# Attention and a feed-forward network on one core: which FFN work lies beside which attention work while the weights are converted

## The chip, the cores and the metric

The kernel runs on one core of a Trainium2 chip. The metric is the device time of one execution in microseconds (us). Matmuls run on TensorE (PE; PEld is its loading of weights); elementwise work on VectorE (DVE), ScalarE (ACT) and GpSimd (POOL); SyncE (SP) issues the DMA transfers.

## The reference

Eight batches of eight heads with 576 tokens of 64 dimensions go through an attention that is causal by blocks of 64 tokens. The result, 4608 tokens of 512 values, goes through two matrix products with a leaky ReLU between them.

```python
scores = scale * np.matmul(q, k.transpose(0, 1, 3, 2))
mask = block_i >= block_j                 # blocks of 64
scores = np.where(mask, scores, -1000000000.0)
attn = np.exp(scores - max) / (sum + 1e-09)
x = (attn @ v).transpose(0, 2, 1, 3).reshape(4608, 512)
h = x @ w_in                              # 512 x 2048
g = np.maximum(0.01 * h, h)
return g @ w_out                          # 2048 x 512
```

q, k and v come as fp32. The weights come as float64, 8 bytes a value, and the kernel makes fp32 of them by integer operations.

## The kernel before, in words

**Split products.** To keep fp32 exactness at the rate of the faster type fp32r, a matrix is cut into a high and a low part, each fp32r, and a product becomes three: high by high, high by low, low by high. The weights have the parts wih, wil, woh and wol; the FFN's input has xh and xl; its middle values have gh and gl; the keys have kh and kl, the probabilities pth and ptl. "Casting" below is making a high part (one copy, L274 on ACT or L275 on DVE), "subtracting" making a low part (L284 on DVE, L285 on POOL).

**Weights.** 64 pieces of 256 columns go through `weight_piece` (L360-419): a load of 8-byte words into one of six `raw` buffers, then steps on `val`, one of six: ACT or DVE scales the upper word, DVE shifts (L397) and ors in the lower word (L401), the sign comes by DVE (L406) or, for every third piece, by ACT and POOL (L410, L411), and a cast and a subtraction give the two parts.

**Attention** (`attention`, L421-665) handles 72 work items. Batch 0 makes 16 of them: items 0 to 7 are its heads' tokens 0 to 319 ("lo"), items 8 to 15 the tokens 320 to 575 ("hi"). From item 16 an item is a whole head ("full"); items 16 to 23 are batch 1. An item loads q, k and v; PE makes scores in the two banks of PSUM called p_s (plain fp32 products L488 for items 0 to 14, the split ones L494 from item 15; every second lo item uses the p_h banks); DVE sets masked corners (memset, L505) and takes maxima (L512, nm), ACT the exponentials (L521, prow), then sums, reciprocals (L535, L536, rec) and normalising (L549 POOL, L550 DVE, L551 ACT); PE transposes the probabilities through the two p_t banks (L573), from which pth and ptl are made; the products with v go back into p_t (L625 plain, L635 split), and copies and adds (L614, L663) put them into xr, the FFN's input by batch. xr of batch 1 lies in memory that the conversion leaves, so it exists only when all weights are there.

**FFN.** 18 chunks of 256 tokens, each in 8 units of 256 columns of the hidden layer. `ffn1` (L723-743) makes 24 matmuls of 256 columns into p_h (L734), then ACT's g (L741), its cast gh and the subtraction gl. `ffn2` (L745-771) makes 12 matmuls of 512 columns into p_o (L753), two banks that sum over all eight units; after the last unit p_o is copied to ob (L770) and stored by SP. Chunk 0 needs the lo items of batch 0, chunk 1 the hi items as well, chunk 2 all of batch 1.

**Order.** No loop fixes the order. Every step is given to `Plan` (L63-234) with its possible engines and their costs, a rank (the number of the item plus an offset of that step's kind) and the buffers that it reads and writes. `Plan.run` plays the program through with its own costs; each engine takes the ready step of lowest rank, and the order that comes out is the program. PE has two rules of its own. A group of transposes ("short") and half an ffn2 unit ("long") that are both ready are put into each other, one matmul of the one, one of the other; and a group of transposes that has no such partner lets other PE work go first for up to PATIENCE ns. Where PE has nothing while work of rank below 12 is open, the plan puts in filler matmuls that nobody reads (L806, 81 of them, two records each).

Chunks 0 and 1 follow one another by rank: chunk 0 spread over items 8 to 15, chunk 1 over 16 to 23, each unit as a step of the items' count. The conversion's ranks run from OFF1 over SL1, also counted in items. Chunk 1's units thereby lie between the scores, transposes and products of batch 1.

Of the kernel before, what the change touches and what calls it, by code (L numbers as in the profile page):

```python
# [17 lines left out]
P = 128  # L18
# [7 lines left out]

HS = 7
SIGNS = 3

WIDE = 256  # L30
RAWS = 6
VALS = 6

RL = 7.153
RP = 0.885
RB = 0.516
RT = 1.485
RV = 1.932
RX = -0.113
RN = -0.908  # L40

LEAD = 1.751
LAG = 1.627
RS = 0.514
RG = -0.26
OFF1 = 4.574
SL1 = 11.938
AHEAD = -0.663

LAT = 1550  # L50
HOLD = 567.499

PATIENCE = 424.599
FILL = 235
# [8 lines left out]
class Plan:  # L63


# [36 lines left out]
    def run(self):  # L102
# [12 lines left out]
        order, now, moved, done = [], 0, 0, 0  # L115
        load, start, stream = -LOAD, 0, 0

# [15 lines left out]

        def multiply(matmuls):
            nonlocal load, start, stream
            for cost, fn in matmuls:
                if now < SLOW:
                    cost *= 2
                load = max(load + LOAD, start, now - 57)
                start = max(start + stream, load + 57, now)  # L140
                stream = cost
                order.append(fn)
            return start + stream

        def best(kind):
            found = [x for x in ready["PE"] if self.ops[x[1]][4] == kind and not ends[x[1]]]
            return min(found) if found else None

# [3 lines left out]
        while done < total:  # L152
# [6 lines left out]
            for e, q in ready.items():  # L159
                while q and ends[q[0][1]]:  # L160
                    heapq.heappop(q)
                if not q or free[e] > now:
                    continue
                other = {"DVE": "POOL", "POOL": "DVE"}.get(e)
                if other:
                    open_ = port[other] <= now
                    can = [x for x in q if not ends[x[1]] and (open_ or (e == "DVE" and self.ops[x[1]][0][x[2]][0] == "DVE"))]
                    if not can:
                        wake.append(port[other])
                        continue  # L170
                    x = min(can)
                    q.remove(x)
                    heapq.heapify(q)
                elif e == "PE":
                    live = [x for x in q if not ends[x[1]]]
                    x = min(live)
                    short, long_ = best("short"), best("long")
                    if self.ops[x[1]][4] == "short" and not long_:
                        other_ = [y for y in live if self.ops[y[1]][4] != "short"]
                        if other_ and now < since[x[1]] + PATIENCE:  # L180
                            x = min(other_)
                    kind = self.ops[x[1]][4]
                    if kind == "long":
                        self.fill = None
                    if kind in ("short", "long") and short and long_:
                        a = [(c, f, short[1]) for c, f in self.ops[short[1]][0][0][1]]
                        b = [(c, f, long_[1]) for c, f in self.ops[long_[1]][0][0][1]]
                        mixed = []
                        while a or b:
# [4 lines left out]
                        at = {}  # L194
                        for c, f, i in mixed:
                            at[i] = multiply([(c, f)])
                        free[e] = start + stream
                        for y in (short, long_):
                            q.remove(y)
                            end(y[1], e, at[y[1]])  # L200
                        heapq.heapify(q)
                        continue
                    q.remove(x)
                    heapq.heapify(q)
                    free[e] = multiply(self.ops[x[1]][0][x[2]][1])
# [12 lines left out]
                order.append(fn)  # L218
                end(i, e, moved + LAT if lag else free[e])
# [38 lines left out]
def attention_ffn(ctx: ExitStack, tc: tile.TileContext, qk: bass.AP, v: bass.AP, w_in: bass.AP, w_out: bass.AP, out: bass.AP):  # L258
# [73 lines left out]
    p_h = fixed([P, 2, CH], F32, "p_h", 2, pool=psum)  # L332
    p_o = fixed([P, DM], F32, "p_o", 2, pool=psum)

# [86 lines left out]
    def attention(i):  # L421
# [10 lines left out]
        sk = "h" if odd else "s"  # L432

        def scored(k):
            return p_h[k].rearrange("p a b -> p (a b)") if odd else p_s[:, k, :]

# [125 lines left out]
        if kind != "lo":  # L562
            softmax(
                [(4, p_s[:, :, 0:288], (0, 1))],
                [(k, (4, p_s[:, k, 0:288], 288 * k, 288 * k + 288, c)) for k in range(2) for c in range(1 if plain_s else 2)],
                [p_s[0:64, 1, 224:288]], r0 + RB,
            )
        for base, c0, w, items in tgroups[kind]:
            x = bank()

            def transpose(t, j, c, x=x):
                n = P if kind == "full" else qn[t]
                return RATE * n, lambda: nc.tensor.transpose(p_t[x][:, c : c + n], row(t, n, j * P, P), ident[:n, :n])  # L573

            add([("PE", [transpose(*y) for y in items])], r0 + RT, [k for t in sorted({a for a, _, _ in items}) for k in pkeys(t)], [("t", x)], kind="short")
            src = p_t[x][:, c0 : c0 + w]
# [128 lines left out]

    def split_x(c, rank):
        at = c * CH
        while at < (c + 1) * CH:
# [13 lines left out]

    def ffn1(c, u, rank):  # L723
        ks = [(a, d) for a in ("xh", "xl") for d in range(0, CH, BLK)]
        hh = p_h[u % 2]
        z = u % 2
        for i in range(2):
            f = 2 * u + i

            terms = [(w, x, d) for d in range(ND) for w, x in ((wih, xh), (wih, xl), (wil, xh))]  # L730

            def go(k, i=i, f=f, terms=terms):
                w, x, d = terms[k]
                nc.tensor.matmul(  # L734
                    hh[:, i, :], w[:, d, f * P : (f + 1) * P], x[:, d, :], start=k == 0, stop=k == len(terms) - 1
                )
# [7 lines left out]

    def ffn2(c, u, rank):  # L745
        z = u % 2
        for m in range(2):

            terms = [(a, w, i) for a, w in ((gh[z], woh), (gh[z], wol), (gl[z], woh)) for i in range(2)]

            def go(k, m=m, terms=terms):
                a, w, i = terms[k]
                nc.tensor.matmul(  # L753
                    p_o[m], a[:, i, m * P : (m + 1) * P], w[:, 2 * u + i, :],
                    start=u == 0 and k == 0, stop=u == NU - 1 and k == 5,
                )

            add(
                [("PE", [(RATE * DM, lambda k=k, go=go: go(k)) for k in range(6)])], rank + m / 1000,
                [("gh", z), ("gl", z)] + wkeys[("wo", 2 * u)] + wkeys[("wo", 2 * u + 1)], [("o", m)], kind="long",  # L760
            )
            if u == NU - 1:
# [6 lines left out]

                add(copying(512, lambda buf=buf: buf, lambda m=m: p_o[m], sb=False), rank, [("o", m)], [key])  # L770
                add([("SP", 475, store)], rank, [key], [("out", c, m)], lag=dma(P * DM * 4))
# [13 lines left out]
    for i in range(len(work) + 1):  # L785
        if i in events:
            here = [c for c in range(NCHUNK) if ready[c] == i]
            nxt = events[events.index(i) + 1] if i != events[-1] else i + H
            num = len(here) * NU
            for k in range(num):  # L790
                c, u = here[k // NU], k % NU
# [3 lines left out]
                ffn1(c, u, rank)  # L795
                ffn2(c, u, rank + (nxt - i) * LAG / num + 0.003)
        if i == 2 * H:
# [5 lines left out]
    if FILL:  # L803

        def fill():
            nc.tensor.matmul(p_o[0][:, 0:P], ident, ident, start=True, stop=True)  # L806

# [29 lines left out]
```

## Time and profile before

| | |
|---|---|
| median of 3 runs | 1193.65 us (1190.58 to 1194.34) |
| profiled execution | 1194.37 us, its span 1192.3 us |
| granted TensorE clock, mean | 0.996 |
| busy: PE, DVE, ACT, POOL | 99%, 57%, 55%, 36% of the span |
| HBM read and written | 64.57 MB and 9.44 MB |

The span is the time from the first to the last recorded instruction; 2.1 us of the execution lie around it. A row of the timeline has start, duration, engine, line, operation, the tiles written and read, shapes and the count of equal instructions, with the idle time of the engine before it in brackets. Matmuls are pipelined: a record is longer than the time from one start to the next. A row of the groups has the count, busy time, mean duration in ns, and after the second bar the idle time in front of them. A row of the windows has the stretch, its length, the busy time of PE, weight loads, DVE, ACT and POOL with their counts, the granted clock, the busy share of the DMA engines and GB/s.

### The profile page before, as it was taken

The page shows a single profiled execution, that of the slowest core. Times are in us where ns is not written, and L with a number is a line of the kernel's source. Part 1 is how long each engine was busy: PE and PEld are TensorE (multiplying, and loading weights), DVE is VectorE, ACT ScalarE, POOL GpSimd, SP SyncE. Part 2 cuts the span into 40 slices and gives each one's busy share as a digit, 9 for nine tenths or more (in the row PEclk, how much of TensorE's full clock was granted, in tenths as well). Part 3 has the DMA queues.
Part 4 walks back from the last instruction along what each step waited for, and adds up shares of the span by engine and source line. Part 5 has one row for each costly group of instructions (what it writes and reads, how often), then busy time and mean ns, then how long its engine had stood idle before and what let it go on. Part 6 is the DMA issues. An engine that isn't in the chain of part 4 may idle for free.

```text
span 1192.3 us, 21079 instructions
## 1 busy us (share of the span) xinstructions
PE 1175.5 (99%) x7778; PEld 1041.4 (87%) x7778; DVE 680.2 (57%) x1782; ACT 657.4 (55%) x1652; POOL 431.5 (36%) x505
## 2 busy tenths in 40 slices
PE   9999899899999999999999999999999999999998
PEld 7877789788899988898999988898998888899997
DVE  5999987766656666644444456665666666310000
ACT  6988866655655565554554455555555555422222
POOL 3233344324443443423332343443444343212222
PEclk9999999899999999999999999999999999999999
DMA  6656422211212111110211211112121210000000
GB/s 175 185 173 193 128 88 72 66 60 55 67 51 70 52 55 60 37 64 30 62 39 35 67 49 55 47 51 69 52 69 46 70 31 30 1 18 1 18 19 18
DMA packets 39592, 75.37 MB, mean 63 GB/s; under 512 B 4032, under 2 KB 23040, under 8 KB 39488
## 3 DMA queue, kind: packets, MB, share of 16 engines
q1 hardware_dynamic: 39488, 74.02, 20.2%
q8 instruction: 61, 1.00, 0.3%
q14 instruction: 43, 0.35, 0.1%
HBM read 64.57 MB, written 9.44 MB: 62 GB/s over the span
## 4 chain that ended last, share of the span: by engine, by line
PE 96%; DVE 2%; ACT 1%; DMA 0%; issue 0%; ACTq 0%; DVEq 0%
PE p_o L753 33%; PE p_h L734 33%; PE p_t L573 9%; PE p_t L635 8%; PE p_s L494 8%; PE p_t L625 2%; PE p_s L488 2%; PE p_o L806 2%; DVE nm L512 1%; PE p_h L488 0%; DVE ptl L284 0%; DVE prow L550 0%; DMA qk_in<-in_qk 0%; ACT prow L521 0%; DMA raw<-in_w_in 0%
## 5 line engine op out<-in xcount | busy, mean ns | idle before, releaser
L285 POOL TENSOR_TENSOR gl<-g,gh 128x512 fp32r<-128x512 f32 x136 | 176.8, 1300 | 460.6 <-ACT gh L274 311.3
L734 PE MATMUL p_h<-xh,wih 128*128 128x256 f32 x1152 | 323.2, 281 | 0.0
L734 PE MATMUL p_h<-xl,wih 128*128 128x256 f32 x1152 | 320.1, 278 | 1.1 <-DVE xl L284 1.1
L734 PE MATMUL p_h<-xh,wil 128*128 128x256 f32 x1152 | 319.9, 278 | 0.0
L521 ACT ACTIVATE prow<-p_s,nm 128x192 f32<-128x192 f32 (+4 forms) x308 | 161.8, 529 | 151.4 <-DVE nm L512 95.4
L573 PE MATMUL p_t<-ident,prow 128*128 128x128 f32 x960 | 239.7, 274 | 3.1 <-DVE ptl L284 0.9
L734 PEld LDWEIGHTS p_h<-xl,wih 128*128 128x128 f32 x1152 | 216.9, 188 | 4.6 <-DVE xl L284 1.3
L734 PEld LDWEIGHTS p_h<-xh,wih 128*128 128x128 f32 x1152 | 216.9, 188 | 4.5 <-issue 1.0
L753 PE MATMUL p_o<-wol,gh 128*128 128x512 f32 x576 | 219.9, 453 | 0.0
L734 PEld LDWEIGHTS p_h<-xh,wil 128*128 128x128 f32 x1152 | 217.0, 188 | 0.0
L741 ACT ACTIVATE g<-p_h 128x512 f32<-128x512 f32 x144 | 85.7, 595 | 234.4 <-PE p_h L734 234.1
L753 PE MATMUL p_o<-woh,gh 128*128 128x512 f32 x576 | 204.0, 426 | 0.0
L753 PE MATMUL p_o<-woh,gl 128*128 128x512 f32 x576 | 192.2, 415 | 0.0
L549 POOL TENSOR_SCALAR prow<-prow,rec 128x192 f32<-128x192 f32 (+4 forms) x214 | 119.1, 568 | 167.1 <-DVE rec L536 124.3
L284 DVE TENSOR_TENSOR ptl<-p_t,pth 128x512 fp32r<-128x512 f32 (+1 forms) x224 | 125.1, 567 | 63.0 <-ACT pth L274 59.6
L614 DVE TENSOR_TENSOR xr<-p_t,xr 64x64 f32<-64x64 f32 x112 | 50.4, 450 | 164.6 <-ACT xr L274 164.3
L573 PEld LDWEIGHTS p_t<-ident,prow 128*128 128x128 f32 x960 | 130.2, 141 | 13.9 <-DVE ptl L284 1.9
L512 DVE TENSOR_REDUCE nm<-p_s 128x1 f32<-128x192 f32 (+4 forms) x308 | 139.7, 486 | 4.6
L753 PEld LDWEIGHTS p_o<-wol,gh 128*128 128x128 f32 x576 | 108.6, 188 | 35.6
L753 PEld LDWEIGHTS p_o<-woh,gh 128*128 128x128 f32 x576 | 105.5, 189 | 28.1 <-issue 2.6
L274 ACT CAST pth<-p_t 128x384 fp32r<-128x384 f32 (+3 forms) x175 | 81.5, 469 | 63.9 <-PE p_t L573 59.5
L753 PEld LDWEIGHTS p_o<-woh,gl 128*128 128x128 f32 x576 | 96.6, 189 | 20.0
(77 smaller groups left out, 1623.9 us busy)
## 6 DMA issues: line engine op xcount, KB each, us to landing
qk_in<-in_qk SPq DMA_DIRECT2D x56, 576.0 KB, 3.7
v_stage<-in_v SPq DMA_DIRECT2D x56, 160.0 KB, 2.2
out<-ob SPq DMA_DIRECT2D x35, 256.0 KB, 2.0
raw<-in_w_in SPq DMA_DIRECT2D x32, 256.0 KB, 3.0
raw<-in_w_out SPq DMA_DIRECT2D x32, 256.0 KB, 3.2
qk_in<-in_qk SPq DMA_DIRECT2D x8, 160.0 KB, 3.0
vf<-in_v SPq DMA_DIRECT2D x8, 160.0 KB, 3.2
vf<-in_v SPq DMA_DIRECT2D x8, 128.0 KB, 2.6
```

The lines of the kernel that those rows point to most:

```text
L274: one = lambda: nc.scalar.copy(dst(), src())
L284: ("DVE+" if sb else "DVE", dve(n), lambda: nc.vector.tensor_sub(dst(), one(), two())),
L285: ("POOL", pool2(n), lambda: nc.gpsimd.tensor_sub(dst(), one(), two())),
L494: go = lambda ap=ap, cols=cols, kk=kk, k0=k0, k1=k1, first=first, last=last: nc.tensor.matmul(ap, qs[z][:, cols], kk[:, k0:k1], start=firs ...
L512: [("DVE", dve(kw[t]), lambda t=t, ap=ap, flat=flat: nc.vector.tensor_reduce(nm[z][: qn[t], t : t + 1], ap[: qn[t]], axis=AX.X if flat els ...
L521: nc.scalar.activation(o, ap[: qn[t]], AF.Exp, bias=nm[z][: qn[t], t : t + 1], scale=1.0, accum_out=sums[z][: qn[t], t : t + 1])
L549: ("POOL", pool1(kw[t]), lambda: nc.gpsimd.tensor_scalar(p(), p(), by, 1.0, op0=ALU.mult, op1=ALU.mult)),
L573: return RATE * n, lambda: nc.tensor.transpose(p_t[x][:, c : c + n], row(t, n, j * P, P), ident[:n, :n])
L635: nc.tensor.matmul(to, vs[z][:, j, :], src, start=start, stop=stop)
L734: nc.tensor.matmul(hh[:, i, :], w[:, d, f * P : (f + 1) * P], x[:, d, :], start=k == 0, stop=k == len(terms) - 1)
L741: add([("ACT", act(512), lambda: nc.scalar.activation(g, hh, AF.Prelu, alpha=0.01))], rank, [("h", z)], ["g"])
L753: nc.tensor.matmul(p_o[m], a[:, i, m * P : (m + 1) * P], w[:, 2 * u + i, :], start=u == 0 and k == 0, stop=u == NU - 1 and k == 5,)
```

## The change

The weights' pieces become 512 columns wide, 32 of them, with three buffers of each kind in place of six; every second one takes its sign from ACT and POOL. The scores of batch 0, in plain fp32 for all 16 items, go into p_o, which is one tile of two banks now; its q and k loads fill all 128 partitions (the inputs hold each row twice), with half the scale, since each product is then summed twice. Chunk 0 sums in p_s instead, takes its split input from space in pth and kl, and so can run while batch 0's last scores use p_o. Chunks 0 and 1 run in step: unit k of chunk 0, then unit k-6 of chunk 1, with ranks tied to the conversion and not to the items. From chunk 2 on the loop is as before, with other offsets. PE takes its lowest rank always: transposes are no longer put between the matmuls of ffn2 and stay together as a group. The planner's second choice of an engine (a cast on DVE, say, where ACT is the first) is allowed after 59 ns in place of 567.

```diff
-HS = 7
-SIGNS = 3
-WIDE = 256
-RAWS = 6
-VALS = 6
+HS = 8
+SIGNS = 2
+WIDE = 512
+RAWS = 3
+VALS = 3
...
+JOINL = 6.278
+LATER = 6
+JOIN = -0.606
+JLAG = 1.738
...
-HOLD = 567.499
-
-PATIENCE = 424.599
+HOLD = 59.027
...
-                    if kind in ("short", "long") and short and long_:
...
-                            if b:
-                                mixed.append(b.pop(0))
-                            if a:
-                                mixed.append(a.pop(0))
...
+                    x = heapq.heappop(q)
...
-    p_o = fixed([P, DM], F32, "p_o", 2, pool=psum)
+    p_o = fixed([P, 2, DM], F32, "p_o", pool=psum)
...
-        rows = D if plain_s else P
+        rows = P
...
+        p_k = p_s if kind == "full" else p_o
...
-            add(copying(qe - qa, lambda: q_in, lambda: q_in, by=scale), rp, [], [qkey])
+            add(copying(qe - qa, lambda: q_in, lambda: q_in, by=scale / 2), rp, [], [qkey])
...
     def split_x(c, rank):
+        if c == 0:
+            x = xr[0][:, :, c * CH : (c + 1) * CH]
+            keys = [("x", 0, h, 0) for h in range(H)]
+            hi = [("pth", y[0]) for y in tgroups["full"]]
+            add(copying(4 * CH, lambda: x2h, lambda: x, first="DVE"), rank, keys, hi)
+            for y in range(2):
+                ds = slice(2 * y, 2 * y + 2)
+                add(subtracting(2 * CH, lambda y=y: x2l[y], lambda ds=ds: x[:, ds], lambda ds=ds: x2h[:, ds]), rank, keys + hi, [("kl", y)])
+            return
...
+            po, po_key = (p_s[:, m, :], ("s", m)) if c == 0 else (p_o[:, m, :], ("o", m))
...
+            if i == 2 * H:
+                steps = [y for k in range(NU + LATER) for y in ((0, k), (1, k - LATER)) if 0 <= y[1] < NU]
+                for k, (c, u) in enumerate(steps):
+                    rank = OFF1 + SL1 * (u + 1) / NU + JOIN + c * JOINL
+                    if u == 0:
+                        split_x(c, (c + 1) * H + JOINX)
+                    ffn1(c, u, k % 2, rank)
+                    ffn2(c, u, k % 2, rank + JLAG)
+                here = []
+            if i == H:
+                here = []
...
-            nc.tensor.matmul(p_o[0][:, 0:P], ident, ident, start=True, stop=True)
+            nc.tensor.matmul(p_s[:, 0, 0:P], ident, ident, start=True, stop=True)
```

By the lines moved, L488 becomes L460, L494 L466, L573 L545, L625 L597, L635 L607, L734 L722, L753 L741, L512 L484, L521 L493, L274 and L275 L245 and L246, L284 and L285 L255 and L256. In the program's order, the lists per engine of before and after, three places show what moves.

PE before, ahead of the first scores of item 16 (the last four rows; p_o_110 is one of the banks in which chunk 0 sums, row L625 an item of batch 0):

```order
L494 MATMUL p_s<-kl_93,qs_89 128x288
L625 MATMUL p_t_107<-ptf,vf_136 64x256 x3
L625 MATMUL p_t_107<-ptf,vf_136 64x192
L625 MATMUL p_t_107<-ptf,vf_136 64x64
L753 MATMUL p_o_110<-woh,gh_113 128x512 x2
L753 MATMUL p_o_110<-wol,gh_113 128x512 x2
L753 MATMUL p_o_110<-woh,gl_115 128x512 x2
L494 MATMUL p_s<-kh_90,qs_88 128x448
L494 MATMUL p_s<-kh_90,qs_88 128x64
L494 MATMUL p_s<-kl_92,qs_88 128x448
L494 MATMUL p_s<-kl_92,qs_88 128x64
```

PE after, at the same place; chunk 0's last sums go into p_s, and twelve matmuls of chunk 1 (three of them shown) stand between these and the scores:

```order
L741 MATMUL p_s<-woh,gh_112 128x512 x2
L741 MATMUL p_s<-wol,gh_112 128x512 x2
L741 MATMUL p_s<-woh,gl_114 128x512 x2
...
L722 MATMUL p_h_108<-xh,wih 128x256
L722 MATMUL p_h_108<-xl,wih 128x256
L722 MATMUL p_h_108<-xh,wil 128x256
L466 MATMUL p_s<-kh_90,qs_88 128x448
L466 MATMUL p_s<-kh_90,qs_88 128x64
L466 MATMUL p_s<-kl_92,qs_88 128x448
L466 MATMUL p_s<-kl_92,qs_88 128x64
```

Chunk 0 is complete ahead of item 16 now, and over half of chunk 1 as well: 300 matmuls of L722 and 120 of L741 stand there where 168 and 78 stood.

PE before, behind the value products of item 22, in batch 1:

```order
L635 MATMUL p_t_106<-pth,vs_94 128x320
L635 MATMUL p_t_106<-ptl,vs_94 128x320
L753 MATMUL p_o_110<-woh,gh_114 128x512 x2
L753 MATMUL p_o_110<-wol,gh_114 128x512 x2
L753 MATMUL p_o_110<-woh,gl_116 128x512 x2
L753 MATMUL p_o_111<-woh,gh_114 128x512 x2
L753 MATMUL p_o_111<-wol,gh_114 128x512 x2
L753 MATMUL p_o_111<-woh,gl_116 128x512 x2
L573 MATMUL p_t_106<-ident,prow_1_1610 128x128
```

PE after, behind those of item 21:

```order
L607 MATMUL p_t_106<-pth,vs_95 128x320
L607 MATMUL p_t_106<-ptl,vs_95 128x320
L466 MATMUL p_s<-kh_91,qs_89 128x448
L466 MATMUL p_s<-kh_91,qs_89 128x64
L466 MATMUL p_s<-kl_93,qs_89 128x448
L466 MATMUL p_s<-kl_93,qs_89 128x64
L466 MATMUL p_s<-kh_91,qs_89 128x320
L466 MATMUL p_s<-kh_91,qs_89 128x192
L466 MATMUL p_s<-kl_93,qs_89 128x320
L466 MATMUL p_s<-kl_93,qs_89 128x192
L545 MATMUL p_t_106<-ident,prow_1_74 128x128
```

The FFN's twelve matmuls between an item's products and the next transposes are gone: from item 20's scores to item 24's PE's list holds scores, transposes and products only.

DVE before, in the same part of the program (one item's rows from its reciprocal on):

```order
L535 TENSOR_SCALAR rec_100<-sums_98 128x4
L536 RECIPROCAL rec_100<-rec_100 128x4
L284 TENSOR_TENSOR ptl<-p_t_106,pth 128x448
L284 TENSOR_TENSOR ptl<-p_t_107,pth 128x512
L505 MEMSET p_s 64x64
L550 TENSOR_SCALAR prow_2_75<-prow_2_75,rec_100 128x320
L512 TENSOR_REDUCE nm_96<-p_s 128x1
L284 TENSOR_TENSOR ptl<-p_t_106,pth 128x256
L284 TENSOR_TENSOR ptl<-p_t_107,pth 128x384
L275 COPY ob<-p_o_111 128x512
```

DVE after:

```order
L255 TENSOR_TENSOR ptl<-p_t_106,pth 128x448
L255 TENSOR_TENSOR ptl<-p_t_107,pth 128x512
L246 CAST pth<-p_t_106 128x256
L255 TENSOR_TENSOR ptl<-p_t_106,pth 128x256
L246 CAST pth<-p_t_107 128x384
L507 TENSOR_SCALAR rec_100<-sums_98 128x4
L508 RECIPROCAL rec_100<-rec_100 128x4
L255 TENSOR_TENSOR ptl<-p_t_107,pth 128x384
L477 MEMSET p_s 64x64
L484 TENSOR_REDUCE nm_96<-p_s 128x1
L246 CAST kh_90<-qk_in_86 128x576
L246 COPY xr_1348<-p_t_107 64x64
```

Two casts of pth, that of kh and a copy of xr, which ACT made before, stand in DVE's list now; the chunk's copy ob is gone from here.

More of the change, by code (lines that the diff above doesn't have):

```diff
@@ L25 @@
 CH = 256
-HS = 7
-SIGNS = 3
-WIDE = 256
-RAWS = 6
-VALS = 6
[L34 to L48, printed above, removed]
+HS = 8
[3 more added lines that the diff above has]
+VALS = 3
+RL = 7.389
+RP = 0.481
+RB = 0.519
+RT = 1.431
+RV = 2.276
+RX = -0.781
+RN = 0.216
+LEAD = 1.579
+LAG = 0.427
+RS = 1.631
+RG = 0.225
+JOINL = 6.278
+LATER = 6
+JOIN = -0.606
+JLAG = 1.738
+JOINX = 6.916
+OFF1 = 9.007
+SL1 = 9.853
+AHEAD = 0.755
 LAT = 1550
-HOLD = 567.499
-PATIENCE = 424.599
+HOLD = 59.027
 FILL = 235
@@ L115, in run @@
         order, now, moved, done = [], 0, 0, 0
[L116 removed]
+        start, stream = 0, 0
         def offer(i):
@@ L132, in end, with multiply @@
                     offer(j)
-        def multiply(matmuls):
-            nonlocal load, start, stream
+        def multiply(matmuls, at):
+            nonlocal start, stream
             for cost, fn in matmuls:
@@ L174, in run @@
                 elif e == "PE":
[L175 to L183, printed above, removed]
-                        self.fill = None
-                    if kind in ("short", "long") and short and long_:
[L186 to L189, printed above, removed]
-                            if b:
-                                mixed.append(b.pop(0))
-                            if a:
-                                mixed.append(a.pop(0))
[L194 to L205, printed above, removed]
+                    x = heapq.heappop(q)
+                    if self.ops[x[1]][4] == "long":
+                        self.fill = None
+                    free[e] = multiply(self.ops[x[1]][0][x[2]][1], since[x[1]])
                     end(x[1], e, free[e])
@@ L429, in attention @@
         plain_s, plain_v = kind == "lo" or kind == "hi" and h < HS, kind != "full"
-        rows = D if plain_s else P
+        rows = P
         odd = kind == "lo" and z == 1
-        sk = "h" if odd else "s"
+        sk = "h" if odd else "s" if kind == "full" else "o"
+        p_k = p_s if kind == "full" else p_o
         def scored(k):
-            return p_h[k].rearrange("p a b -> p (a b)") if odd else p_s[:, k, :]
+            return p_h[k].rearrange("p a b -> p (a b)") if odd else p_k[:, k, :]
         def row(t, n, c, w):
@@ L563, in attention @@
             softmax(
-                [(4, p_s[:, :, 0:288], (0, 1))],
-                [(k, (4, p_s[:, k, 0:288], 288 * k, 288 * k + 288, c)) for k in range(2) for c in range(1 if plain_s else 2)],
-                [p_s[0:64, 1, 224:288]], r0 + RB,
+                [(4, p_k[:, :, 0:288], (0, 1))],
+                [(k, (4, p_k[:, k, 0:288], 288 * k, 288 * k + 288, c)) for k in range(2) for c in range(1 if plain_s else 2)],
+                [p_k[0:64, 1, 224:288]], r0 + RB,
             )
@@ L572, in transpose @@
                 n = P if kind == "full" else qn[t]
-                return RATE * n, lambda: nc.tensor.transpose(p_t[x][:, c : c + n], row(t, n, j * P, P), ident[:n, :n])
-            add([("PE", [transpose(*y) for y in items])], r0 + RT, [k for t in sorted({a for a, _, _ in items}) for k in pkeys(t)], [("t", x)], kind="short")
+                return 27, lambda: nc.tensor.transpose(p_t[x][:, c : c + n], row(t, n, j * P, P), ident[:n, :n])
+            add([("PE", [transpose(*y) for y in items])], r0 + RT, [k for t in sorted({a for a, _, _ in items}) for k in pkeys(t)], [("t", x)])
             src = p_t[x][:, c0 : c0 + w]
@@ L721, in split_x, with ffn1 @@
             at += ln
[L723 to L726, printed above, removed]
+    x2h = pth[:, 0 : ND * CH].rearrange("p (d t) -> p d t", d=ND)
+    x2l = [kl[y][:, 0 : 2 * CH].rearrange("p (d t) -> p d t", d=2) for y in range(2)]
+    def ffn1(c, u, z, rank):
+        if c == 0:
+            ks = [("pth", y[0]) for y in tgroups["full"]] + [("kl", 0), ("kl", 1)]
+            xs = [(x2h[:, d], x2l[d // 2][:, d % 2]) for d in range(ND)]
+        else:
+            ks = [(a, d) for a in ("xh", "xl") for d in range(0, CH, BLK)]
+            xs = [(xh[:, d], xl[:, d]) for d in range(ND)]
+        hh = p_h[z]
         for i in range(2):
             f = 2 * u + i
-            terms = [(w, x, d) for d in range(ND) for w, x in ((wih, xh), (wih, xl), (wil, xh))]
+            terms = [(w, xs[d][x], d) for d in range(ND) for w, x in ((wih, 0), (wih, 1), (wil, 0))]
             def go(k, i=i, f=f, terms=terms):
```

24 lines of the change are left out of this document (10 added, 14 removed).

## The prediction

> **What bounds the kernel now.** I read the page first: span, busy times, the chain that ended last.
>
> ```profile
> PE 1175.5 (99%) x7778; PEld 1041.4 (87%) x7778; DVE 680.2 (57%) x1782; ACT 657.4 (55%) x1652; POOL 431.5 (36%) x505
> ...
> PE p_o L753 33%; PE p_h L734 33%; PE p_t L573 9%; PE p_t L635 8%; PE p_s L494 8%; PE p_t L625 2%; PE p_s L488 2%; PE p_o L806 2%; DVE nm L512 1%; PE p_h L488 0%; DVE ptl L284 0%; DVE prow L550 0%; DMA qk_in<-in_qk 0%; ACT prow L521 0%; DMA raw<-in_w_in 0%
> ```
>
> TensorE is the bound. The 1728 matmuls of L753 take 33% of the span of 1192.3 us, or 0.228 us each from start to start; the 3456 of L734 take 0.114 us each. The change leaves their number alone, so it can only touch time in which PE does something else: filler matmuls, waits, a lowered clock, transposes. The windows say where such time is.
>
> ```profile
> core 0 of [0], span 1192.3 us
> core 0: us, PE busy (x) PEld busy (x) DVE busy (x) ACT busy (x) POOL busy (x), PEclk, DMA share, GB/s
> 59.90:131.40 71.50, 70.69 (x407) 54.71 (x407) 65.37 (x188) 60.26 (x156) 24.17 (x28) 1.00 0.62 190
> 220.00:250.00 30.00, 24.05 (x125) 20.18 (x124) 22.91 (x62) 19.46 (x54) 11.90 (x17) 0.83 0.23 74
> 217.50:238.70 21.20, 17.55 (x93) 14.58 (x91) 16.75 (x47) 13.86 (x39) 7.44 (x11) 0.84 0.17 57
> 400.00:600.00 200.00, 200.00 (x1357) 179.75 (x1355) 112.84 (x281) 106.24 (x264) 71.97 (x83) 1.00 0.17 51
> ```
>
> Behind 250 us PE doesn't wait (400 to 600 us: busy throughout). Before that two stretches lose most: the start, held by fillers, and 220 to 250 us (6 us idle, and a clock of 0.83, worth 5 us more). From 60 to 130 us, with the weights' conversion at its height, PE idles 0.8 us of 71.5. So nearly all that could be won lies in the fillers and in 220 to 250 us.
>
> I cut the program at three marks: A, the first FFN matmul; B, the first score matmul of item 16 (batch 1); C, the first matmul of chunk 2, which needs all of batch 1.
>
> ```profile
> 59.94 0.38 PE L734 MATMUL p_h<-xh,wih 128*128 128x256 f32 x1
> ...
> 131.47 0.39 PE L494 MATMUL p_s<-kh,qs 128*128 128x448 f32 x2
> ...
> 244.16 0.36 PE L734 MATMUL p_h<-xh,wih 128*128 128x256 f32 x1
> ```
>
> **Up to A.** The fillers fall from 81 to 62; each is two of these records.
>
> ```profile
> L806 PE MATMUL p_o<-ident 128*128 128x128 f32 x131 | 17.2, 277 | 0.0
> ```
>
> ```profile
> 62.88 1.95 PE L625 MATMUL p_t<-ptf,vf 128*64 128x256 f32 x10
> ```
>
> Between 20 and 60 us, where they go, one costs 17.2 / 65.5 = 0.26 us; 19 fewer save 5.0 us. One item's value product (the second row), behind A before, now stands ahead of it: 1.9 us. A moves from 59.9 to 56.8 us, if the fillers that stay cover what is waited for, as they do now. Bounds: 52 to 60.
>
> **A to B.** By the program's order PE has here 168 matmuls of L734 and 78 of L753 before, 300 and 120 after: chunk 0 now ends ahead of B, because it sums in the score banks, and more than half of chunk 1's L734 goes with it. Before, FFN work is 168 x 0.114 + 78 x 0.228 = 37.0 us; the other 33.7 us of the 70.7 busy ones are scores, transposes and products of the first batch. After, the FFN is 34.2 + 27.4 = 61.6 us; the others gain nine transposes and item 15's scores in plain fp32, about 2 us: 35.8. With the same 0.8 us of idle time B comes at 56.8 + 98.2 = 155.0 us, 23.5 later. Nothing is lost by that alone; the work is moved.
>
> The conversion lies beside this. Each of its steps on DVE, ACT and POOL halves in number and pays its fixed part once for twice the columns; that is work of DVE and ACT behind a PE that idles 0.8 us, so worth nothing beyond the fillers. Three buffers of 512 KB hold as much as six of 256. The query and key loads of batch 0 read 128 partitions instead of 64 (for item 15 it was 128 already), nearly 3 MB more on SP's queue; at 190 GB/s that is 15 us of transfer in 130 us with the DMA engines 62% busy, which I take as hidden. If the loads fell behind, PE would wait at A or later, with chunk 0's FFN behind it: 0 to 10 us, taken at 0. Batch 0's scores in p_o queue behind nothing, since chunk 1 enters p_o only after them. Item 16's scores now wait for chunk 0's last copy out of p_s; twelve matmuls of L734 and four scores stand between, 1.9 us, against one copy of about 0.7 us and its hand-overs: nothing, and at most 1 us.
>
> **B to C.** Here the FFN that lay over batch 1's attention is thinner: 216 matmuls of L734 and 114 of L753 before (50.6 us), 84 and 72 after (26.0 us), all but twelve of these ahead of item 20's scores. From there to item 24 PE has attention alone: scores, transposes, scores, products. What one item takes on PE follows from the chain by line above: L573 9%, L635 8% and L494 8% of 1192.3 us, over 64, 56 and 57 items, are 1.7 us each; the percentages are rounded, and I take 4.9 us for the three, 1.65 of it scores. How often an item comes when PE is not the bound is seen where the kernel before is nearly bare, items 23 to 25:
>
> ```profile
> 216.41 0.39 PE L494 MATMUL p_s<-kh,qs 128*128 128x448 f32 x2
> ...
> 226.38 0.80 PE L494 MATMUL p_s<-kh,qs 128*128 128x448 f32 x2 [1.67 <-ACT prow L521]
> ...
> 228.63 0.79 PE L635 MATMUL p_t<-pth,vs 128*128 128x512 f32 x2
> ...
> 234.88 1.03 PE L573 MATMUL p_t<-ident,prow 128*128 128x128 f32 x8
> 235.67 0.38 PE L494 MATMUL p_s<-kh,qs 128*128 128x288 f32 x1
> ...
> 238.69 0.82 PE L635 MATMUL p_t<-pth,vs 128*128 128x512 f32 x2 [0.67 <-DVE ptl L284]
> ...
> 240.65 0.39 PE L494 MATMUL p_s<-kh,qs 128*128 128x448 f32 x2
> ```
>
> Scores start 10.0 and then 14.3 us apart, products 10.1. The chain is scores, maxima, exponentials, normalising, transposes, casts, products, with one pair of score banks and one of transpose banks, and DVE carries 16.75 us (217.5 to 238.7 us) for two items, 8.4 each. After, DVE gets more of an item:
>
> ```profile
> L275 DVE CAST pth<-p_t 128x512 fp32r<-128x512 f32 (+1 forms) x49 | 33.5, 685 | 58.2 <-PE p_t L573 58.0
> ...
> L284 DVE TENSOR_TENSOR xl<-xr,xh 128x1024 fp32r<-128x1024 f32 (+3 forms) x23 | 21.3, 944 | 0.4
> ...
> L275 DVE COPY ob<-p_o 128x512 f32<-128x512 f32 x2 | 1.4, 686 | 0.2 <-PE p_o L753 0.2
> L275 DVE CAST kh<-qk_in 128x576 fp32r<-128x576 f32 x2 | 1.2, 576 | 0.0
> ```
>
> Added for an item: the kh cast 0.58, two casts of pth (256 and 384 columns, under the 0.69 of the wider ones: 1.0 for both), two copies of xr (512 and 64 columns: 0.69 and 0.2). Gone are what those two items had besides: one gl of ob's width, two ob, xl with its cast, about 3 us, 1.5 an item. So 8.4 + 2.5 - 1.5 = 9.4 us. At DVE's share in that window (79%) an item takes 11.9 us, at the 91% it has from 60 to 130 us 10.3. I take 11.0; bounds 8.4 (DVE as now, never waiting) and 14.3.
>
> B to item 20's scores: 84 x 0.114 + 60 x 0.228 + attention (6.6 of scores, three items of 3.2) = 39.5 us of PE for four items; with attention at 10 to 11 us an item, 43. Then five items of 11.0, and 3.5 us from item 25's scores to C, as now (240.65 to 244.16). C = 155.0 + 43 + 55 + 3.5 = 256.5 us, 12.3 later than before. PE's wait returns as one block of some 30 us in place of the fillers and the 220 us stretch.
>
> **Behind C.** 705 transposes stood one by one between matmuls of L753; now they come in groups.
>
> ```profile
> 605.85 0.40 PE L753 MATMUL p_o<-woh,gh 128*128 128x512 f32 x1
> ...
> 607.68 0.40 PE L753 MATMUL p_o<-woh,gh 128*128 128x512 f32 x1
> ```
>
> Six of L753 and four transposes take 1.83 us, so a transpose costs (1.83 - 6 x 0.228) / 4 = 0.115 us. Grouped, eight take 0.79 us (234.88 to 235.67) and delay the score behind them by 0.08: 0.109. The gain is 705 x 0.006 = 4 us; twice an item a score now precedes L734 where it was once, a few hundredths of a us each time, so I take -3 (-4 to 0). Other steps move between DVE, ACT and POOL under a PE that never waits: +1 (0 to +4).
>
> **Sum.** +12.3 - 3 + 1 = +10 us on the profiled execution's 1194.4 us, which is 0.7 above the median of the three runs: 1204.
>
> **Rivals.**
> *No new wait* (faster). If attention kept up with PE, B to C would shrink by the FFN taken out of it (24.6 us) and item 15's product and transposes (2.9): C = 155.0 + 112.7 - 27.5 = 240.2, 4 us earlier, and -3 behind it: 1187. It decides at 8.4 us an item. For it: POOL's normalising mostly goes, and DVE may run freer of POOL:
>
> ```profile
> L471 DVE SCALAR_TENSOR_TENSOR qs<-qk_in,qs 64x576 fp32r<-64x576 f32 (+1 forms) x57 | 75.9, 1332 | 1.8
> ```
>
> ```profile
> 240.00 0.76 DVE L471 SCALAR_TENSOR_TENSOR qs<-qk_in,qs 64x576 fp32r<-64x576 f32 x1
> ```
>
> This step takes 0.76 us alone, 1.33 on average. Against it: the three bare intervals above are 10.0 us and more. Chance 0.14. [...]
>
> *A little faster items* (no change). At 9.8 us an item and 40 us to item 20, C = 247.5, +3.3 - 3: 1194. Chance 0.17.
>
> *Half clock all through* (slower still). With the clock at 0.84 in the bare window and waits of 1.7 us at most, a whole stretch of such items could stay low; at 14.3 us an item and 46 to item 20, C = 276: 1224. Chance 0.12. [...]
>
> *The weights fall behind* (three large buffers, more bytes). PE waits before B: +10 more, 1214. Chance 0.07.
>
> **The numbers.** Forecast 0.50, between 1199 and 1213. The range takes in the no-change case and part of each end: 1190 to 1218. A measurement of this kernel tells 0.3% (3.6 us) from no change. Faster by more: 0.14 and a little of the no-change case, 0.16. Within: 0.15. Slower: 0.69.
>
> **What would show it.** Fillers near 18 us, A near 57, B near 155, C near 256; a clock under 0.9 from about 198 to 260 us with PE idle there for 20 us or more; score starts of items 20 to 25 near 11 us apart; DVE over 80% busy there. PE full from 265 us on. C before 245 would break the forecast; so would PE waits between A and B.

## The result, and the profile after

The changed kernel takes 1221.76 us (median of 4 runs, 1219.44 to 1223.71), against 1192.99 for the kernel before in the same series: a ratio of 1.0243, 95% interval 1.0217 to 1.0268. The forecast was 1204 with a range to 1218: the sign was right, the size was not. The profiled execution has a span of 1221.9 us, 29.6 more than before.

The page of the changed kernel: busy time, then the chain that ended last.

```profile
PE 1184.0 (97%) x7740; PEld 1062.1 (87%) x7740; DVE 787.5 (64%) x1915; ACT 638.0 (52%) x1556; POOL 298.6 (24%) x268
...
PE 74%; DVE 18%; ACT 4%; issue 3%; DMA 1%; SPq 0%; POOL 0%; ACTq 0%; POOLq 0%; DVEq 0%
PE p_o L741 30%; PE p_h L722 20%; PE p_t L607 7%; DVE qs L443 6%; PE p_s L466 6%; PE p_t L545 6%; DVE nm L484 3%; ACT prow L493 3%; DVE ptl L255 3%; DVE pth L246 2%; PE p_t L597 1%; PE p_s L741 1%; PE p_o L460 1%; PE p_s L806 1%; DVE p_s L477 1%
```

PE's share of the chain fell from 96% to 74%, and one DVE step, L443, which the chain's list of before does not name, has 6% of it, some 73 us. That is too much for the bare stretch alone (205 to 255.7 us, where the attention of batch 1 has no FFN beside it). The three marks of the prediction, in the timeline:

```profile
58.45 0.36 PE L722 MATMUL p_h<-pth,wih 128*128 128x256 f32 x1
...
154.73 0.40 PE L466 MATMUL p_s<-kh,qs 128*128 128x448 f32 x2
...
255.75 0.56 PE L722 MATMUL p_h<-xh,wih 128*128 128x256 f32 x1
```

A, B and C were forecast at 56.8, 155.0 and 256.5 us. C is 11.6 us later than before (12.3 forecast). Behind C lie 966.2 us, where before had 948.1: 18.1 us more, where the prediction had 2 less. The whole miss in the sum is there. The windows of the same three parts:

```profile
58.40:154.70 96.30, 95.58 (x592) 79.90 (x591) 76.54 (x151) 68.50 (x132) 31.10 (x29) 1.00 0.55 172
205.00:255.70 50.70, 35.34 (x166) 27.51 (x166) 46.35 (x121) 30.12 (x79) 14.25 (x14) 0.79 0.24 75
400.00:600.00 200.00, 198.40 (x1327) 181.40 (x1327) 132.38 (x325) 102.76 (x257) 45.85 (x38) 1.00 0.16 50
```

The first row idles 0.7 us of 96.3, as forecast. The second is the bare stretch: PE busy 70%, DVE 91%, a clock of 0.79. In the third, PE makes 1327 matmul records in 200 us where before made 1357, and DVE's busy time rose from 112.8 to 132.4 us. Where the time goes is seen in the chain of waits of a single item there (start, length, step):

```profile
506.82 0.61 DVE ptl L255
507.43 0.00 issue
507.43 0.11 DVE p_s L477
507.54 0.03 issue
507.57 2.00 DVE qs L443
509.58 0.02 issue
509.60 0.77 DVE nm L484
510.37 0.02 issue
510.39 0.84 ACT prow L493 x2
511.23 0.04 issue
511.28 1.39 PE p_s L466 x8
```

Read it from below. The 448-column scores of the next item wait for the exponentials (L493) to leave the score banks, those wait for the maximum over 576 columns (L484), and that one stands on DVE behind the qs step of an item two further on (L443), which nobody needs yet. That step takes 2.00 us. POOL's timeline says why:

```profile
507.54 1.42 POOL L256 TENSOR_TENSOR kl<-qk_in,kh 128x576 fp32r<-128x576 f32 x1 [4.00 <-ACT kh L245]
```

The kl subtraction started on POOL 0.03 us ahead of DVE's step; each of the two reads two tiles. Over 300 to 1000 us the step has these means, before (L471) and after (L443):

```profile
L471 DVE SCALAR_TENSOR_TENSOR qs<-qk_in,qs 64x576 fp32r<-64x576 f32 x41 | 58.3, 1423 | 1.3
```

```profile
L443 DVE SCALAR_TENSOR_TENSOR qs<-qk_in,qs 64x576 fp32r<-64x576 f32 x40 | 69.5, 1738 | 1.2
```

Before, too, it was often long, but it stood elsewhere: behind C, 38 of 47 of those maxima came right behind the masks (L505) on DVE, and after, 37 of 47 come right behind a qs step. And PE had more to do between an item's 288-column scores and the next 448-column ones: their starts lay 8.4 us apart (median), now 5.9 with the wait in it. After, scores follow directly on L722 in 41 places behind C: from that L722 to the score the starts lie 0.446 us apart on the mean, 0.115 where nothing waits, so 41 x 0.331 = 13.6 us of waiting. The waits view books 7.8 of it as idle time of PE; the rest lies under the last L722's own record, which is 0.28 us long:

```profile
PE p_s L466 <- ACT prow L493: 7.8, 34, 0.3
```

### The profile page after: what moved, and what is told of

The parts are those of the page before. It is cut to its first block, busy times and chain, and to the rows that moved or that the text cites. A ratio compares the mean times of both kernels' runs of the same rounds, so it can differ in the third digit from the quotient of the medians.

```text
span 1221.9 us, 20601 instructions
## 1 busy us (share of the span) xinstructions
PE 1184.0 (97%) x7740; PEld 1062.1 (87%) x7740; DVE 787.5 (64%) x1915; ACT 638.0 (52%) x1556; POOL 298.6 (24%) x268
## 4 chain that ended last, share of the span: by engine, by line
PE 74%; DVE 18%; ACT 4%; issue 3%; DMA 1%; SPq 0%; POOL 0%; ACTq 0%; POOLq 0%; DVEq 0%
PE p_o L741 30%; PE p_h L722 20%; PE p_t L607 7%; DVE qs L443 6%; PE p_s L466 6%; PE p_t L545 6%; DVE nm L484 3%; ACT prow L493 3%; DVE ptl L255 3%; DVE pth L246 2%; PE p_t L597 1%; PE p_s L741 1%; PE p_o L460 1%; PE p_s L806 1%; DVE p_s L477 1%
## 5 line engine op out<-in xcount | busy, mean ns | idle before, releaser
L722 PE MATMUL p_h<-xh,wih 128*128 128x256 f32 x1088 | 309.1, 284 | 0.0
L722 PE MATMUL p_h<-xl,wih 128*128 128x256 f32 x1088 | 303.4, 279 | 0.6 <-DVE xl L255 0.6
L722 PE MATMUL p_h<-xh,wil 128*128 128x256 f32 x1088 | 302.7, 278 | 0.0
L722 PEld LDWEIGHTS p_h<-xl,wih 128*128 128x128 f32 x1088 | 205.6, 189 | 2.5 <-DVE xl L255 1.4
L722 PEld LDWEIGHTS p_h<-xh,wih 128*128 128x128 f32 x1088 | 205.6, 189 | 1.1
L722 PEld LDWEIGHTS p_h<-xh,wil 128*128 128x128 f32 x1088 | 205.4, 189 | 0.0
L256 POOL TENSOR_TENSOR gl<-g,gh 128x512 fp32r<-128x512 f32 x90 | 117.6, 1307 | 359.2 <-ACT gh L245 319.1
L493 ACT ACTIVATE prow<-p_s,nm 128x448 f32<-128x448 f32 x280 | 144.0, 520 | 90.6 <-DVE nm L484 90.4
L741 PE MATMUL p_o<-woh,gh 128*128 128x512 f32 x544 | 169.8, 393 | 0.0
L741 PE MATMUL p_o<-wol,gh 128*128 128x512 f32 x544 | 169.6, 393 | 0.0
L741 PE MATMUL p_o<-woh,gl 128*128 128x512 f32 x544 | 169.6, 393 | 0.0
L545 PE MATMUL p_t<-ident,prow 128*128 128x128 f32 x960 | 136.2, 280 | 19.8 <-DVE xr L586 6.8
L545 PEld LDWEIGHTS p_t<-ident,prow 128*128 128x128 f32 x960 | 112.3, 144 | 37.5 <-DVE xr L586 7.7
L245 ACT CAST pth<-p_t 128x384 fp32r<-128x384 f32 (+2 forms) x154 | 71.7, 494 | 126.6 <-PE p_t L545 125.0
L484 DVE TENSOR_REDUCE nm<-p_s 128x1 f32<-128x448 f32 x280 | 121.7, 479 | 3.5
L741 PEld LDWEIGHTS p_o<-woh,gl 128*128 128x128 f32 x544 | 102.3, 188 | 23.1
L741 PEld LDWEIGHTS p_o<-wol,gh 128*128 128x128 f32 x544 | 102.2, 188 | 22.6
L255 DVE TENSOR_TENSOR ptl<-p_t,pth 128x512 fp32r<-128x512 f32 (+1 forms) x224 | 118.2, 566 | 2.6 <-ACT pth L245 0.4
L256 POOL TENSOR_TENSOR kl<-qk_in,kh 128x576 fp32r<-128x576 f32 x54 | 78.5, 1454 | 161.3 <-ACT kh L245 150.2
L741 PEld LDWEIGHTS p_o<-woh,gh 128*128 128x128 f32 x544 | 94.6, 188 | 12.7 <-ACT ob L245 0.2
L256 POOL TENSOR_TENSOR vs<-v_stage,vs 128x320 fp32r<-128x320 f32 x54 | 48.5, 897 | 229.8 <-DVE vs L246 219.6
```

The lines of the kernel that those rows point to most:

```text
L245: one = lambda: nc.scalar.copy(dst(), src())
L255: ("DVE+" if sb else "DVE", dve(n), lambda: nc.vector.tensor_sub(dst(), one(), two())),
L256: ("POOL", pool2(n), lambda: nc.gpsimd.tensor_sub(dst(), one(), two())),
L484: [("DVE", dve(kw[t]), lambda t=t, ap=ap, flat=flat: nc.vector.tensor_reduce(nm[z][: qn[t], t : t + 1], ap[: qn[t]], axis=AX.X if flat els ...
L493: nc.scalar.activation(o, ap[: qn[t]], AF.Exp, bias=nm[z][: qn[t], t : t + 1], scale=1.0, accum_out=sums[z][: qn[t], t : t + 1])
L545: return 27, lambda: nc.tensor.transpose(p_t[x][:, c : c + n], row(t, n, j * P, P), ident[:n, :n])
```

## The experiments

Two theories for the miss. **Theory 1:** DVE's qs step and POOL's kl collide, and the qs step stands ahead of the maximum, so the exponentials are late and PE waits. **Rival:** the grouped transposes cost more, or leave too little work between an item's two sets of scores. For the bare stretch: theory 2 (half the clock: 0.50 was granted from 232 to 236 us), theory 3 (no FFN beside it), and DVE's own pace. Where an edit works on the finished order, it moves instructions in the list that the planner made, and everything else stays in its place.

**Maxima first.** DVE's order alone is changed:

```diff
+        for it in range(2 * H + 1, len(work)):
+            x, y = find("qs", it), find("nm", 4, it - 2)
+            if y is not None and x < y:
+                order.insert(y, order.pop(x))
```

> Only DVE's order differs from the changed kernel: the 576-column maximum stands ahead of the next item's qs step, and kl still runs on POOL beside that. Theory 1: the exponential comes 2 us earlier, the wait goes though the qs step stays at 1.7 us: 1209 us. If it is DVE's load and not the place of one step that counts, qs comes late in its turn and the scores wait for it: 1220 us.

Measured: 1203.99 us (1202.99 to 1206.69), ratio 1.0089 [1.0073, 1.0104]. Its DVE in the same phase of an item:

```profile
498.09 0.11 DVE L481 MEMSET p_s<- 64x64 f32 x1
498.24 0.76 DVE L488 TENSOR_REDUCE nm<-p_s 128x1 f32<-128x576 f32 x1
499.03 1.20 DVE L447 SCALAR_TENSOR_TENSOR qs<-qk_in,qs 64x576 fp32r<-64x576 f32 x1
```

The maximum comes at once, the waits for L493 are gone from the view, and C (254.79 us) to the end takes 946.8 us: 19.4 less than the changed kernel and 1.3 less than before. Of the 19.4, 13.6 are the wait itself and 3.8 the scores behind it, whose weight loads the wait had held back too (PEld waited 14.8 us there in all, in 35 places); the rest is scattered. One edit on DVE's order gives the forecast's part behind C nearly to the number (-2 forecast, -1.3 measured).

**kl behind qs.** The second way: POOL copies one column of qs, and so waits for it, ahead of every kl that POOL makes.

```diff
+                order.insert(max(x, y), ((-2, 0), lambda it=it: nc.gpsimd.tensor_copy(poke, qs[it % 2][64:128, 0:1])))
```

> The orders of PE, DVE, ACT and SP stay as in the changed kernel; POOL copies one column of qs ahead of each kl subtraction, so that it can't run beside DVE's qs step. Theory 1 (the two steps collide, DVE's qs step takes 1.74 us in place of 0.76 and makes the maxima, the exponentials and so the next scores late, 0.33 us an item on 41 items): the qs step falls to about 0.8 us, PE no longer waits in front of the 448-column scores behind chunk 2's start, 13 us less: 1209 us, the part behind C near 953 us in place of 966. Rival (grouped transposes and too little cover between the two sets of scores): the qs step gets shorter, PE's time behind C stays within 3 us: 1220 us.

Measured: 1214.66 us. The wait was gone (0.1 us of 13.6 left), yet only 7 us with it: each L722 stood 117.4 ns behind the last one, to the very end of the program, where no such copy runs, and where before and after have 113.3. All 126 units behind C had the slow spacing; in the changed kernel 37 of 127 have it, taking a mean over 115.5 ns for slow. The scratch tile had moved the tiles behind it. A larger scratch did not mend it:

> As kl_behind_qs, only the scratch tile of the copy is 128 bytes a partition in place of 4, which moves the tiles behind it in memory by 128 bytes. In kl_behind_qs the wait was gone, but matmuls of L722 stood 117.4 ns apart through the whole program, to its very end, where before and after have 113.3. Theory (the 4 bytes moved the FFN's operands off an even address): 113.3 ns again, 1203 us, like max_before_qs or a little better for the bare stretch. Rival (the copies on POOL slow PE): 117.4 ns stays, 1214 us.

Measured: 1214.96 us, spacing 117.5 ns: neither an even 128 bytes nor the smaller tile keeps the fast spacing. Next, the tile without the copies:

```diff
+    poke = fixed([64, 1], F32, "poke")
+    nc.gpsimd.memset(poke, 0.0)
```

> max_before_qs with a tile of 4 bytes a partition in the place where kl_behind_qs has its scratch, set once and not used. If the place of the tiles behind it is what makes each FFN matmul 4 ns longer: 117.5 ns and 1214 us. If it is the 55 copies on POOL: 113.3 ns and 1204 us, as max_before_qs.

Measured: 1221.17 us, 17 more than max_before_qs without the tile. The windows of the last part of the program, where only the FFN runs, without the tile and with it (PE's records in 80 us):

```profile
1090.00:1170.00 80.00, 80.00 (x535) 73.11 (x534) 5.05 (x6) 20.61 (x35) 16.76 (x13) 1.00 0.04 14
```

```profile
1090.00:1170.00 80.00, 80.00 (x506) 71.88 (x505) 5.05 (x6) 18.33 (x31) 15.45 (x12) 1.00 0.02 7
```

PE is busy throughout and its clock full in both, and makes 5% fewer records (they mix both matmul widths, so the spacing is the surer figure). So the copies are cleared, and the second way was tried once more with the scratch behind all other tiles:

> kl_behind_qs with its scratch of 4 bytes behind all other tiles, so that no other tile moves; from item 19 on. If the place of the tiles is what kept the FFN's matmuls 117.5 ns apart, and the wait alone is worth some 19 us behind C and 5 us ahead of it: 113.4 ns, 1199 us. If the copies on POOL cost it: 1214 us again.

Measured: 1198.48 us (1196.34 to 1200.34), ratio 1.0035 [1.0021, 1.0049]. The qs step over 300 to 1000 us, and POOL around one:

```profile
L448 DVE SCALAR_TENSOR_TENSOR qs<-qk_in,qs 64x576 fp32r<-64x576 f32 x41 | 31.5, 769 | 1.3
```

```profile
509.49 0.18 POOL L821 CAST poke<-qs 64x1 fp32r<-64x1 f32 x1 [4.89 <-DVE qs L448]
509.75 1.44 POOL L260 TENSOR_TENSOR kl<-qk_in,kh 128x576 fp32r<-128x576 f32 x1
```

With no overlap the step takes 0.77 us, and kl 1.44, as in the changed kernel. Behind C there are 947.9 us, 18.3 less than the changed kernel; B to C takes 96.5 in place of 101.0. Two edits that share nothing but this chain give the same 18 to 19 us: theory 1 is shown, and its rival refuted behind C. The second leaves the qs step ahead of the maximum, and at 0.77 us it does no harm there: the place and the collision were both needed.

**The tile in the kernel before.**

> The kernel before with an unused tile of 4 bytes a partition ahead of kl, and nothing else. If the place alone costs 4 ns a matmul in this program too: 117.5 ns, 15 to 17 us more, 1209 us. If it was an accident of the changed kernel's program: within 2 us of before.

Measured: 1208.66 us, ratio 1.0119 [1.0096, 1.0141]: an unused tile of 4 bytes a partition costs some 14.6 us here too. The same windows, of before and with the tile:

```profile
1090.00:1170.00 80.00, 80.00 (x523) 72.71 (x522) 3.84 (x4) 20.31 (x34) 20.09 (x15) 1.00 0.04 14
```

```profile
1090.00:1170.00 80.00, 80.00 (x510) 72.13 (x509) 3.84 (x4) 19.81 (x33) 19.19 (x15) 1.00 0.04 14
```

**Grouped transposes by themselves**, in the kernel before:

```diff
+                        plain = [f for _, f, _ in b + a]
...
+                        order[len(order) - len(plain) :] = plain
```

> The kernel before with its plan as it was, only that where four transposes stood between six matmuls of L753, the six come first and the four behind them. This is the prediction's term behind C by itself (705 transposes by 0.006 us): 3 to 4 us less than before, 1190.5 us. Rival (grouping gains nothing on PE): within 1.5 us of before. Second rival (transposes that come up to 0.9 us later make PE wait for pth and ptl): more than before.

Measured: 1194.46 us against 1193.35, ratio 0.9996 [0.9973, 1.0019]; in the profiled execution C came 2.1 us earlier and the rest took 2.4 more. Nothing can be measured, as the first rival has it; but the interval reaches from 3.2 us less to 2.3 us more, so the time alone doesn't rule out the forecast 3. The trace says more. Counted from start to start, the transposes and L753 behind C take 9.5 us less than in before, the scores 3.7 more and L734 8.2 more. Of these 8.2, 5.2 lie in single steps of over 130 ns, most of them right behind a group; most of the rest is the slow spacing again, in 48 of 125 units where before has 25 of 126. What the group saves, the matmuls behind it pay.

**A held clock**, with fillers in the bare stretch:

> Twelve filler matmuls (0.24 us each) more in each of items 21 to 24, in front of their transposes, where PE waits; all else as in the changed kernel. Theory 2 (half the clock makes PE's part of the chain longer in the bare stretch: 11.5 to 12.1 us an item against 8.8 for the one at full clock): clock 1.0 from 205 to 250 us, items near 9.5 us, C about 8 us earlier, 1213 us. Rival (DVE's chain sets the pace and PE's clock is hidden): C within 2 us of 255.8, 1221 us.

Measured: 1217.9 us. The window of the stretch:

```profile
205.00:255.70 50.70, 41.91 (x276) 34.86 (x275) 46.60 (x122) 30.83 (x85) 13.45 (x12) 0.97 0.21 70
```

The clock rose from 0.79 to 0.97, but C came at 251.4, 2.8 of the 4.4 us being an earlier A; B to C took 99.4 in place of 101.0. The lowered clock cost 1.6 us, not 8, net of what the fillers themselves may have delayed, which no run separates. That PE's pace was hidden behind DVE is the likely reading: DVE is busy 43.3 of the 46.4 us up to C.

**Chunk 1 in the common loop.**

```diff
-                steps = [y for k in range(NU + LATER) for y in ((0, k), (1, k - LATER)) if 0 <= y[1] < NU]
+                steps = [(0, k) for k in range(NU)]
...
-                here = []
```

> Chunk 1 goes back into the common loop, its eight units spread over items 16 to 23; chunk 0 stays in step with the conversion in the score banks. Theory 3 (batch 1's attention is bare since chunk 1 went ahead): B near 140, C near 246 us, no bare stretch: about 10 us less, 1211 us. Rival (the attention of batch 1 is slow by its own chain, whatever lies beside it): C within 3 us of 255.8, 1221 us.

Measured: 1219.75 us, C at 251.4. It hardly spread: PE takes what is ready, and 288 matmuls of L722 still stand ahead of B (300 in the changed kernel). B to C took 96.8 us in place of 101.0. But the new order also parted qs and kl there: the last six qs steps between B and C take 0.76 us each, where the last four of the changed kernel take 1.9, so the 4.2 us can be the collision's, like the 4.5 of kl_behind_qs_late. Inconclusive on theory 3, so the banks were put back as well:

> The changed kernel with batch 0's scores in p_s and chunk 0's sums in p_o, as before the change, and so chunk 1 behind chunk 0 (LATER = 8). Theory (item 16's scores come 23 us late because chunk 0 holds p_s until the last weights are there; from B on an item takes 10 to 12 us by DVE's chain whatever lies beside it): B near 132, C near 244, 1209 us. Rival (B waits for the weights or for memory, not for the banks): B within 5 us of 154, 1221 us.

Measured: 1215.59 us; B at 138.3, C at 253.2. Item 16 started 16 us earlier, but with FFN work beside them items 20 to 24 took 12.2 us each in place of 11.1, and C gained 2.6. That the banks delay B holds; that this is what C loses does not.

**Fewer steps for DVE.**

> The changed kernel with HOLD at 567 as before, so that the planner gives a step to its second engine less readily: DVE loses casts of pth, vs and kh and subtractions of gl to ACT and POOL. Theory (the 2.5 us that DVE took on for an item set the pace of the bare stretch): items 20 to 24 near 10 us in place of 11.1, B to C about 94 us in place of 101, and less of the wait behind C: 1210 us. Rival (the chain of one score bank pair and one transpose pair sets the pace): 101 us and 1221.

Measured: 1216.81 us; B at 161.5, C at 264.7, B to C 103.2. B came 6.8 us later. From item 20's scores to item 25's an item took 10.7 us in place of 11.1, though DVE's busy time in it fell from 10.1 us to 8.4, so the steps that DVE took on are not what sets the pace there by themselves. Behind C it gained (951.7 us), since the collision went the other way round. The qs and kl steps over 300 to 1000 us:

```profile
L443 DVE SCALAR_TENSOR_TENSOR qs<-qk_in,qs 64x576 fp32r<-64x576 f32 x41 | 33.5, 816 | 1.1
```

```profile
L256 POOL TENSOR_TENSOR kl<-qk_in,kh 128x576 fp32r<-128x576 f32 x41 | 72.0, 1756 | 108.3 <-ACT kh L245 107.7
```

In 36 of 40 overlaps here qs starts first, and takes 0.76 us while kl takes 1.79; in the changed kernel kl starts first in 36 of 37, and takes 1.42 us while qs takes 1.85. In both kernels the second to start paid.

**Narrow pieces.**

```diff
-SIGNS = 2
-WIDE = 512
-RAWS = 3
-VALS = 3
+SIGNS = 3
+WIDE = 256
+RAWS = 6
+VALS = 6
```

> The changed kernel with the conversion as before: 64 pieces of 256 columns, six buffers of each kind, every third sign by ACT and POOL. By the prediction the wide pieces are worth nothing on PE beyond fillers: C within 2 us of that of the changed kernel, 1222 us. Rival (their fixed parts are on the path): A to C 5 us longer, 1227 us.

Measured: 1239.57 us, 18 more than the changed kernel. B came at 174.8, and the waits of PE ahead of it have a row that the changed kernel has not:

```profile
PE p_h L722 <- ACT wih L245: 16.1, 1, 16.1
```

One wait of 16 us for a piece of w_in. The wide pieces, with their buffers and signs, are worth that much in this order of work; which of the three edited things it is, this run doesn't tell.

**Together.**

> Chunk 1 in the common loop (as spread), the 576-column maxima ahead of the qs step from item 27 on only, and the fillers of held_clock. If the three gains add: C near 248, 942 us behind it, 1197 us. If the bare stretch takes no more than one of them: 1202 us.

Measured: 1199.55 us (10 runs), ratio 1.0047 [1.0026, 1.0067]; C 250.2, 945.7 us behind it.

> joined, and for items 19 to 26 kl waits on POOL for DVE's qs step (scratch behind all other tiles). If the collision costs the bare stretch the 5 us that kl_behind_qs showed there: C near 245, 1195 us, level with before. If the fillers and the common loop have taken that already: 1199 us.

Measured: 1201.52 us, C 253.5: kl behind qs added nothing to the stretch (98.5 us from B to C against 98.1), since in joined the last six qs steps before C take 0.76 us already; and B came 2.9 us later. The two runs' times overlap (1199.47 to 1203.77, and 1197.65 to 1202.6).

> HOLD at 567, the maxima ahead of the qs step from item 27 on, and the fillers of held_clock, chunk 1 in step with chunk 0 as in the changed kernel. If DVE's added steps set the pace and the order of DVE the wait behind C: C near 247, 1196 us; else 1203 us.

Measured: 1210.39 us, C 258.6: the late B of the hold run stayed (161.8). No version here beats the kernel before; the two best, kl_behind_qs_late and joined, are 0.3 to 0.5% above it.

## Why the prediction was wrong, point by point

- **Up to A, right:** 58.4 for 56.8; in the edits that leave this part alone A lies between 55.6 and 58.3.
- **A to B, right:** 96.3 us for 98.2, PE idle 0.7 for 0.8. One reason in it was wrong: that the wider pieces are worth nothing beyond fillers. In this order they carry some 20 us (C at 276.3 without them); the forecast came out since the change has both. Twice the columns do take less than twice the time: DVE's shift of `val` took 0.335 us for 256 columns before (L397) and 0.501 for 512 after (L368), the step that ors in the lower word 0.434 and 0.762 (L401, L372).
- **B to C, right:** 101.0 us for 101.5. The score starts 206.15, 214.91, 227.07, 238.53 and 250.61 us are 11.1 us apart, 11.0 forecast:

```profile
206.15 0.50 PE L466 MATMUL p_s<-kh,qs 128*128 128x448 f32 x2 [0.85 <-ACT prow L493]
...
250.61 0.60 PE L466 MATMUL p_s<-kh,qs 128*128 128x448 f32 x2
```

The size is in part luck. The prediction worked out 9.4 us of DVE an item and chose 11.0 between 10.3 and 11.9. In kl_behind_qs_late, with the collision gone, DVE has 9.3 us and an item takes 10.3; in the changed kernel the collision, which the prediction did not count, makes that 10.1 and 11.1. The parts were also off against each other: 40.6 us to item 20's scores for 43, and 5.1 from item 25's to C for 3.5.

- **Behind C, wrong, and this is the step that failed:** "Other steps move between DVE, ACT and POOL under a PE that never waits: +1 (0 to +4)." It measured +19.4, the difference between the changed kernel and max_before_qs. PE does wait. The score banks come free through DVE and ACT, and one DVE step ahead of the maximum, made 1.2 us longer by its neighbour on POOL, was enough; at 0.77 us in the same place it cost nothing. PE's slack was some 0.8 us, an estimate from the item shown above: its step is 1.23 us longer, and PE waits 0.39. The prediction asked of DVE how much it does, and only in the bare stretch; behind C it did not look at what stands ahead of the maximum, though the program's order shows it.
- **The transposes, probably wrong in size:** -3 forecast, no difference in before_grouped, though its interval doesn't exclude 3. The prediction priced a group up to its last start and let the matmuls behind it pay too little: 9.5 us saved, 11.9 paid.
- **The rivals:** 1221.8 lies near the 1224 of "half clock all through", but not by its mechanism: C was to come at 276 and came at 255.8, and the held clock gave 1.6 us. "The weights fall behind" did not happen: PE idles 0.7 us from A to B. "No new wait" counted on DVE running freer of POOL. POOL does slow the qs step: in the kernel before, the 24 of 576 columns with POOL idle beside them take 0.76 us each, and the 27 that start while POOL is at kl take 1.92 on the mean. But the change goes the other way: it moves kl to POOL (54 of 56 items, before 33 of 57), beside the qs step, which takes 2.00 us where kl began 0.03 us earlier, against 0.77 where kl waits for it (kl_behind_qs_late). In the hold run kl is the one that pays: 1.79 us, against the 1.44 of kl_behind_qs_late.

What stays open: the rest of the pace in the bare stretch (10.3 us an item with the collision gone, 9.3 of them DVE's, and by the prediction's estimate 4.9 of them PE's).

## What to carry to other kernels

When steps move between engines behind a saturated PE, ask of each engine not only how busy it is but what it has queued ahead of the step that frees PE's next bank; a step nobody needs yet, put there, cost here what it exceeded the slack by: nothing at 0.77 us, and 0.39 us of wait in the item with 2.00. A pair of steps like qs on DVE and kl on POOL, 1.85 and 1.42 us where kl started first and 0.77 and 1.44 apart, should be given an order. And an experiment that adds a tile should put it behind all others: ahead of kl, an unused tile cost 17.2 and 14.6 us here by itself.

## What the runs showed of the hardware that was not expected

An unused tile of 4 bytes a partition, ahead of kl, made the spacing of the 256-column FFN matmuls 117.5 ns in place of 113.3 through whole programs: 17.2 us in max_first_tile against max_before_qs, 14.6 in before_tile. The same tile behind all others (kl_behind_qs_late) cost nothing that shows: PE has 520 records from 1090 to 1170 us, the changed kernel 524, and max_first_tile, with the tile ahead of kl, 506. In kernels without it both spacings occur too. The timeline of before, at the first of 24 matmuls of L734 and at what follows the last, for two units that follow one another:

```profile
603.02 0.28 PE L734 MATMUL p_h<-xh,wih 128*128 128x256 f32 x1
...
605.85 0.40 PE L753 MATMUL p_o<-woh,gh 128*128 128x512 f32 x1
...
609.92 0.28 PE L734 MATMUL p_h<-xh,wih 128*128 128x256 f32 x1
...
612.65 0.45 PE L635 MATMUL p_t<-pth,vs 128*128 128x512 f32 x2
```

That is 2.83 us and 2.73 us for 24, or 118 and 114 ns, with all tiles at fixed places. In the hold run, which adds no tile, all 21 units behind 1090 us are slow, at 117.7 ns; in the changed kernel, from which it differs by one threshold of the planner, one of 22 is. So the place bears on how often the slow spacing holds, but the order of the work does too, and the cause is open.
